# Threshold attention and a squared-ReLU FFN: two hand-written step orders of the attention stage replaced by two others

## The chip, the cores and the metric

The kernel runs on one core of one Trainium2 chip. A core has five engines with a queue each: TensorE (PE: matmuls and transposes; its weight loads are shown as PEld), VectorE (DVE), ScalarE (ACT), GpSimd (POOL) and SyncE (SP, which issues nearly all transfers here). Each engine works through its own instructions in the order in which the program gives them and waits, where it must, on semaphores that the other engines or transfers raise. The metric is the device time of one execution in microseconds (us); the times before were taken in 3 runs.

## The reference

```python
# q, k, v: (8, 8, 576, 64) float32; tau = 0.02
scores = scale * np.matmul(q, k.transpose(0, 1, 3, 2))
thresh = np.max(scores, axis=-1, keepdims=True) - tau
scores = np.where(scores >= thresh, scores, -1000000000.0)
scores = scores - np.max(scores, axis=-1, keepdims=True)
attn = np.exp(scores)
attn = attn / (np.sum(attn, axis=-1, keepdims=True) + 1e-09)
x = np.matmul(attn, v)             # rearranged to (4608, 512)
h = np.maximum(x @ w_in, 0.0)      # w_in (512, 2048)
out = h * h @ w_out                # w_out (2048, 512)
```

`w_in` and `w_out` arrive as 64-bit floats and are turned into 32-bit floats on the chip, with integer operations on the two halves of each number.

## The kernel before

The attention stage comes first (to about 500 us), then two layers of the FFN, whose matrix products use a scheme of sums and differences of blocks that saves multiplications. The change touches the attention stage alone.

**Units and periods.** 8 batches by 4 pairs of heads give 32 pairs; a pair has 576 queries in four tiles of 128 and one of 64, and the last tiles of two pairs share one unit: 144 units of 128 queries. A *period* p handles two units, A and B, of two heads each (j = 0 and 1), so there are 72 full periods with a few partial ones around them. The work is a software pipeline: a period makes the scores and softmax weights of its own units, transposes most of the weights of the period before (fills V and W), the rest of the weights of the one before that (fill U), and multiplies those with the values (PV).

**Steps.** A period is a list of short names, and the function `period` runs the step of each name in the order of the list. Each step appends its instructions to the queues of its engines, so the list sets the order on every engine at once; what stands in different queues is held together by the waits alone (the whole is under a manual schedule). The names:

| step | engine | what it does | line before |
|---|---|---|---|
| SA, SB | PE | scores of unit A and the last 64 keys of both; scores of B, into PSUM `sc` | L434 |
| T | PE | transposes of queries or keys to come, into two banks of `sc` | L398 |
| eT | ACT | copies these out; SP then loads later queries or keys | L403, L411 |
| U, V, W | PE | transposes of softmax weights (W also spreads the reciprocal sums, L515) | L380 |
| eU, eV, eW | ACT | copies these out | L523 |
| PV | PE | weights by values, into banks 0 and 5 of `sc` | L532 |
| topA0 ... topB1 | DVE | reads 576 scores from PSUM, writes them to SBUF, keeps the extreme of each row | L452 |
| leastA, leastB | POOL | adds tau to that extreme (128x2) | L459 |
| powA0 ... powB1 | ACT | exponential | L462 |
| maskA0 ... maskB1 | DVE | compares scores with the threshold, multiplies with the exponentials, sums rows; both inputs in SBUF | L467 |
| over | POOL | adds 1e-9 to the row sums of the period before (needs its last mask) | L474 |
| inv | DVE | reciprocal of these (128x4) | L477 |
| x | DVE in plain periods, ACT in converting ones | takes the product from PSUM (two instructions) | L659, L657 |
| xm | POOL in converting periods | multiplies x with the reciprocals (L669); in all periods, SP's stores of x and loads of values | L669, L578 |
| fetch | SP | loads a chunk of 64-bit weights | L191 |
| c1 | ACT | first step of the conversion of a chunk | L205 |
| c2, c3 | POOL | second and third, on the two halves | L212, L219 |
| c4, c5 | DVE | fourth and fifth, one period later | L227, L235 |
| c6 | POOL | adds the halves (needs c5) | L245 |
| s1, s2 | POOL | one sum of weight blocks each, 128x512 (a few of x at the end) | L122, L125 |

Chunks begin in periods 2 to 33, and a chunk's second half of steps falls in the next period, so periods 2 to 34 are *converting* and use the list `CONVERTING`; the others use `PLAIN`. In plain periods the steps c1 to c6 and fetch do nothing. s1 and s2 do something only from period 36 on: s2 to period 59, s1 until its sums are done (44 of weights and 12 of x, so until period 67). Periods 0 and 1 have lists of their own.

**What sets the order around it.** Besides the waits on data, `touch` adds waits between engines that use the same PSUM bank, so that, for instance, a top in bank 1 waits for the transposes T that the list has put ahead of it in that bank. The masks wait for their exponential and for least; V waits for all masks of the period before; W waits for inv and for the tops of B; the next SA waits for x, the next SB for eW.

Of the kernel before, what the change touches and what calls it, by code (L numbers as in the profile page):

```python
# [48 lines left out]
def kernel(  # L49
# [438 lines left out]
    for g in range(2, 2 * len(pairs)):  # L488
        two, x = divmod(g - 4, 4)
# [99 lines left out]
    def begun(n):  # L589
        return starts.get(n)  # L590

    PLAIN = """
        SA c3 T topA0 over U eU s1 SB topA1 powA1 leastA topB0 powB0 c1 s2 PV c4 V fetch
        inv powA0 c5 topB1 powB1 eT maskA1 x xm W eV maskA0 leastB c2 c6 eW maskB0
        maskB1
    """.split()
    CONVERTING = """
        fetch SA U eU T SB topA0 s1 c1 topA1 topB0 c3 V PV leastA over powA0 topB1
        powA1 powB0 c4 eT inv x maskA1 maskA0 W leastB maskB0 c5 eV c2 powB1 c6 eW maskB1 xm
    """.split()  # L600

    BEGIN_WITH = {
# [740 lines left out]
```

## Time and profile before

| what | value |
|---|---|
| three runs | 1298.58, 1299.42 (median), 1301.99 us |
| profiled execution | span 1298.2 us from the first to the last instruction; of its own time only this span is shown |
| busy share of the span | PE 98%, PEld 86%, DVE 78%, POOL 71%, ACT 65% |
| granted TensorE clock | mean 0.997; 1.00 from 25 us on |
| converting periods 3 to 34 begin (topA0) | 30.03 to 250.54 us |
| plain periods 36 to 59 begin | 263.72 to 415.21 us; period 60 at 421.66 |
| last mask ends | 500.15 us |

A row of the page gives the line, engine, operation, tiles and shapes, the count, then busy time in us and the mean duration of one in ns, then the idle time of the engine just before them. A timeline gives start, duration, engine, line, operation. On DVE a recorded duration overlaps the start of the next instruction, so the pace of a chain is read from start to start. The rows of DVE_READ_ACCUMULATOR belong to the top or mask before them.

### The profile page before, as it was taken

How to read it: one execution, taken by the hardware profiler on the slowest of the kernel's cores; microseconds unless marked ns; L12 is line 12 of the kernel's file. 1: busy time of each engine (PE TensorE's matmuls, PEld its weight loads, DVE VectorE, ACT ScalarE, POOL GpSimd, SP SyncE). 2: the span in 40 equal slices, each digit the busy share in tenths (PEclk: the TensorE clock that was granted, in tenths of full speed). 3: DMA queues.
4: the chain of work that ended last, by engine and by line, in shares of the span. 5: the costliest groups of instructions: out<-in, count | busy, mean ns of one | idle time of the engine just before them, and what ended most of it. 6: DMA issues, size and time to landing. Idle time of an engine off the chain costs nothing.

```text
span 1298.2 us, 45819 instructions
## 1 busy us (share of the span) xinstructions
PE 1276.4 (98%) x18287; PEld 1117.7 (86%) x18287; DVE 1007.0 (78%) x2423; ACT 845.5 (65%) x1498; POOL 926.8 (71%) x1031
## 2 busy tenths in 40 slices
PE   8999999999999999999999999999999999999998
PEld 5777777677777778988888888999999999999998
DVE  6999999999999996886887878867646654665463
ACT  6999999888998984666765856675523432343240
POOL 2787878755555321888897989858787767777775
PEclk8999999999999999999999999999999999999999
DMA  5665566544333312667768768589554224522411
GB/s 143 163 160 154 153 192 180 149 103 110 85 79 80 92 34 64 191 183 218 212 186 226 218 175 235 162 304 391 195 159 164 83 86 159 163 80 88 160 34 34
DMA packets 291413, 196.20 MB, mean 151 GB/s; under 512 B 100096, under 2 KB 252160, under 8 KB 291200
## 3 DMA queue, kind: packets, MB, share of 16 engines
q1 hardware_dynamic: 289888, 192.87, 51.5%
q8 instruction: 144, 2.36, 0.8%
q14 instruction: 69, 0.57, 0.2%
q10 hardware_dynamic: 1312, 0.41, 0.1%
HBM read 120.85 MB, written 72.35 MB: 149 GB/s over the span
## 4 chain that ended last, share of the span: by engine, by line
PE 86%; ACT 5%; DVE 4%; DMA 3%; issue 2%; POOL 0%; SPq 0%; ACTq 0%; DVEq 0%; POOLq 0%
PE po L1077 28%; PE ph L935 16%; PE sc L532 11%; PE sc L434 10%; PE ph L942 10%; PE pt L380 6%; DVE arena L452 2%; PE sc L515 2%; PE sc L398 2%; ACT arena L462 1%; ACT arena L523 1%; DMA g<-arena 1%; PE sc L380 1%; DVE arena L125 1%; DMA wall<-w 1%
## 5 line engine op out<-in xcount | busy, mean ns | idle before, releaser
L125 POOL TENSOR_TENSOR arena<-arena 128x512 f32<-128x512 f32 (+1 forms) x314 | 378.1, 1222 | 147.0 <-DVE arena L125 119.3
L1077 PE MATMUL po<-wall,arena 128*128 128x128 f32 x3528 | 395.0, 275 | 1.9 <-ACT arena L752 1.4
L1077 PEld LDWEIGHTS po<-wall,arena 128*128 128x128 f32 x3528 | 394.4, 192 | 2.5 <-ACT arena L752 1.8
L125 DVE TENSOR_TENSOR arena<-ph,arena 128x512 f32<-128x512 f32 x378 | 255.1, 689 | 79.9 <-PE ph L935 31.5
L122 POOL TENSOR_TENSOR arena<-arena 128x128 f32<-128x128 f32 (+1 forms) x322 | 265.4, 825 | 23.0 <-DMA arena<-w 6.6
L935 PE MATMUL ph<-arena,wall 128*128 128x256 f32 x1176 | 256.6, 380 | 1.8 <-DVE arena L125 1.4
L935 PEld LDWEIGHTS ph<-arena,wall 128*128 128x128 f32 x1176 | 222.2, 190 | 35.9 <-DVE arena L125 5.4
L125 DVE TENSOR_TENSOR arena<-po,arena 128x128 f32<-128x128 f32 x378 | 108.2, 290 | 167.7 <-PE po L1077 163.4
L467 DVE SCALAR_TENSOR_TENSOR arena<-arena 128x576 f32<-128x576 f32 x288 | 235.7, 855 | 0.9 <-ACT arena L462 0.9
L791 ACT COPY c<-arena 128x512 f32<-128x512 f32 (+1 forms) x295 | 169.0, 578 | 71.8 <-DVE arena L122 35.8
L452 DVE TENSOR_SCALAR_CACHE_REDUCE arena<-sc 128x576 f32<-128x576 f32 x288 | 205.1, 748 | 10.9 <-ACT arena L523 4.3
L462 ACT ACTIVATE arena<-arena 128x576 f32<-128x576 f32 x288 | 208.7, 773 | 7.4 <-DVE arena L452 4.2
L532 PEld LDWEIGHTS sc<-arena 64*64 64x64 f32 x5760 | 159.2, 133 | 36.5 <-DVE arena L452 19.8
L532 PE MATMUL sc<-arena 64*64 64x128 f32 (+1 forms) x5760 | 180.5, 262 | 2.9 <-DVE arena L452 1.3
L434 PE MATMUL sc<-arena 64*64 64x64 f32 (+1 forms) x2304 | 176.2, 415 | 3.8 <-ACT arena L403 2.4
L523 ACT COPY arena<-pt 128x1024 f32<-128x1024 f32 x144 | 146.4, 1016 | 27.9 <-PE pt L380 26.5
L122 DVE TENSOR_TENSOR arena<-arena,c 128x512 f32<-128x512 f32 x235 | 154.4, 666 | 11.0 <-ACT c L791 7.6
L752 ACT COPY arena<-po 128x128 f32<-128x128 f32 x63 | 16.6, 264 | 186.4 <-PE po L1077 183.7
L942 PE MATMUL ph<-arena,wall 128*128 128x128 f32 x1176 | 132.0, 275 | 0.7 <-DVE arena L659 0.7
L942 PEld LDWEIGHTS ph<-arena,wall 128*128 128x128 f32 x1176 | 131.6, 192 | 1.1 <-issue 0.8
L380 PEld LDWEIGHTS pt<-ident,arena 64*128 64x128 f32 x2304 | 83.5, 139 | 40.0 <-ACT arena L523 30.1
L434 PEld LDWEIGHTS sc<-arena 64*64 64x64 f32 x2304 | 74.0, 134 | 42.2 <-issue 14.1
(54 smaller groups left out, 1079.7 us busy)
## 6 DMA issues: line engine op xcount, KB each, us to landing
arena<-g SPq DMA_DIRECT2D x144, 256.0 KB, 4.4
g<-arena SPq DMA_DIRECT2D x192, 128.0 KB, 2.9
w<-arena SPq DMA_DIRECT2D x60, 256.0 KB, 2.8
wall<-w SPq DMA_DIRECT2D x49, 256.0 KB, 5.2
g<-arena SPq DMA_DIRECT2D x48, 256.0 KB, 3.8
arena<-w SPq DMA_DIRECT2D x44, 256.0 KB, 3.3
arena<-in_v_dram SPq DMA_DIRECT2D x32, 288.0 KB, 3.8
out_dram<-arena SPq DMA_DIRECT2D x70, 128.0 KB, 2.2
```

Source lines behind the costliest of these rows:

```text
L122: e.tensor_tensor(out=out, in0=x, in1=y, op=ALU.subtract)
L125: e.tensor_tensor(out=out, in0=x, in1=y, op=ALU.add)
L380: made = nc.tensor.transpose(pt[:, r, ts(slot, HALF)], of[rows, :], ident[rows, rows])
L434: made = nc.tensor.matmul(sc[at, ds(to, count)], lhs, kT[rows, ds(at_k, count)], start=True, stop=True)
L452: made = nc.vector.tensor_scalar(out=s[:, j, :], in0=sc[:, ds(at, S)], scalar1=1.0, scalar2=None, op0=ALU.mult, op1=ALU.min, accum_out=nmx ...
L462: nc.scalar.activation(out=w[:, :, j, :], in_=of(j), func=AF.Exp, bias=nmx[:, j : j + 1], scale=-1.0)
L467: nc.vector.scalar_tensor_tensor(out=w[:, :, j, :], in0=of(j), scalar=thr[:, j : j + 1], in1=w[:, :, j, :], op0=ALU.is_le, op1=ALU.mult, a ...
L532: made = nc.tensor.matmul(sc[ds(u * D, D), ds(5 * j * BANK + row, count)], loaded_v[i][rows, (c - (u != j)) % CH, :], wT[m][rows, ds(weigh ...
L791: nc.scalar.copy(c, y)
L935: nc.tensor.matmul(to[:, 2 * j : 2 * j + 2, :], W_IN[m, k][:, ts(2 * h + j, P)], part_x(steps, k, m), start=(not more and j == 0), stop=Tr ...
L942: nc.tensor.matmul(to[:, j, :], W_IN[m, k][:, ts(j, P)], x, start=(not more and j == 0), stop=True, skip_group_check=True,)
L1077: nc.tensor.matmul(to, g[:, j, :], w[:, j, :], start=(not more and j == 0), stop=(j == 3), skip_group_check=True)
```

## The change

The lists `PLAIN` and `CONVERTING` get another order. Both hold the same steps as before, none is added or left out, and no step does anything else than it did. (All lines of the kernel behind the lists move up by three.)

```diff
     PLAIN = """
-        SA c3 T topA0 over U eU s1 SB topA1 powA1 leastA topB0 powB0 c1 s2 PV c4 V fetch
-        inv powA0 c5 topB1 powB1 eT maskA1 x xm W eV maskA0 leastB c2 c6 eW maskB0
-        maskB1
+        s1 T SA topA0 U topA1 leastA SB eU powA1 PV topB0 over powA0 V topB1 eT maskA1 powB0 inv powB1 maskA0 W eV x s2 leastB maskB0 xm maskB1 eW fetch c4 c5 c6
     """.split()
     CONVERTING = """
-        fetch SA U eU T SB topA0 s1 c1 topA1 topB0 c3 V PV leastA over powA0 topB1
-        powA1 powB0 c4 eT inv x maskA1 maskA0 W leastB maskB0 c5 eV c2 powB1 c6 eW maskB1 xm
+        fetch SA U eU T SB c1 s1 topA0 V powA0 topA1 leastA powA1 PV c4 topB0 powB0 topB1 eT maskA0 c3 x over inv leastB maskA1 c2 c5 W maskB0 eV c6 powB1 xm maskB1 eW
     """.split()
```

The new PLAIN list names c4 to c6 but not c1 to c3, which do nothing there. Read engine by engine (c steps left out in plain periods, where they are empty):

| engine | plain before | plain after |
|---|---|---|
| PE | SA T U SB PV V W | T SA U SB PV V W |
| DVE | topA0 topA1 topB0 inv topB1 maskA1 x maskA0 maskB0 maskB1 | topA0 topA1 topB0 topB1 maskA1 inv maskA0 x maskB0 maskB1 |
| ACT | eU powA1 powB0 powA0 powB1 eT eV eW | eU powA1 powA0 eT powB0 powB1 eV eW |
| POOL | over s1 leastA s2 leastB | s1 leastA over s2 leastB |

| engine | converting before | converting after |
|---|---|---|
| PE | SA U T SB V PV W | the same |
| DVE | topA0 topA1 topB0 topB1 c4 inv maskA1 maskA0 maskB0 c5 maskB1 | topA0 topA1 c4 topB0 topB1 maskA0 inv maskA1 c5 maskB0 maskB1 |
| ACT | eU c1 powA0 powA1 powB0 eT x eV powB1 eW | the same |
| POOL | c3 leastA over leastB c2 c6 xm | leastA c3 over leastB c2 c6 xm |

## The prediction

> **What bounds the kernel now.** I read first the busy time of the engines in two stretches of the attention stage, then the groups of instructions by form in the same stretches, then the timelines of VectorE (DVE) and GpSimd (POOL) in single periods. The granted clock is 1.00 in both stretches.
>
> ```profile
> core 0: us, PE busy (x) PEld busy (x) DVE busy (x) ACT busy (x) POOL busy (x), PEclk, DMA share, GB/s
> 30.00:235.00 205.00, 201.27 (x4952) 150.72 (x4946) 204.39 (x549) 197.71 (x357) 163.53 (x201) 1.00 0.64 168
> 257.00:408.00 151.00, 149.02 (x3926) 111.76 (x3930) 146.03 (x438) 136.22 (x213) 87.01 (x115) 1.00 0.41 95
> ```
>
> In the converting stretch DVE is never idle: its chain sets the period, 7.07 us from one topA0 to the next in most of them (107.76 to 114.85, say). In the plain stretch TensorE is the busier (149.02 of 151), and DVE idles 5 us. From topA0 of period 36 (263.72) to that of period 60 (421.66) are 24 periods of 6.58.
>
> So what counts is what makes a DVE step longer. The masks are not equally long in the two stretches:
>
> ```profile
> L467 DVE SCALAR_TENSOR_TENSOR arena<-arena 128x576 f32<-128x576 f32 x116 | 101.0, 905 | 0.6 <-ACT arena L462 0.6
> ...
> L467 DVE SCALAR_TENSOR_TENSOR arena<-arena 128x576 f32<-128x576 f32 x149 | 116.0, 815 | 0.0
> ```
>
> The timeline of one converting period tells why (DVE first, then POOL):
>
> ```profile
> 103.83 0.78 DVE L467 SCALAR_TENSOR_TENSOR arena<-arena 128x576 f32<-128x576 f32 x1
> ...
> 104.54 1.20 DVE L467 SCALAR_TENSOR_TENSOR arena<-arena 128x576 f32<-128x576 f32 x1
> ...
> 105.68 0.81 DVE L467 SCALAR_TENSOR_TENSOR arena<-arena 128x576 f32<-128x576 f32 x1
> ...
> 106.42 0.69 DVE L235 SCALAR_TENSOR_TENSOR arena<-arena 128x512 int32<-128x512 int32 x1
> 107.02 0.81 DVE L467 SCALAR_TENSOR_TENSOR arena<-arena 128x576 f32<-128x576 f32 x1
> ...
> 104.06 2.02 POOL L212 TENSOR_SCALAR arena<-arena 128x512 int32<-128x512 uint32 x1
> 107.25 1.48 POOL L245 TENSOR_TENSOR wall<-arena 128x512 int32<-128x512 int32 x1 [1.18 <-DVE arena L235]
> ```
>
> c2 (L212) starts 0.23 after maskA1, and it is the next mask, begun while c2 is under way, that takes 1.20 for 0.81: it is held 0.40. c6 (L245) starts 0.23 after maskB1, and maskB1 keeps its 0.81. So who is first at the port goes first, and the other waits. Two more rows give sizes. In period 2 a mask starts 0.215 behind xm (L669) and takes 1.13, held 0.32; in a plain period maskA1 starts 0.95 after a sum of weights (L122) and is held 0.14, so that L122 holds a mask off until about 1.09 after its own start:
>
> ```profile
> 28.97 1.13 DVE L467 SCALAR_TENSOR_TENSOR arena<-arena 128x576 f32<-128x576 f32 x1 [0.61 <-ACT arena L462]
> ...
> 28.75 0.73 POOL L669 TENSOR_TENSOR arena<-arena 128x256 f32<-128x256 f32 x1
> ...
> 306.15 0.95 DVE L467 SCALAR_TENSOR_TENSOR arena<-arena 128x576 f32<-128x576 f32 x1
> ...
> 305.20 1.28 POOL L122 TENSOR_TENSOR wall<-wall 128x512 f32<-128x512 f32 x1
> 306.46 0.80 POOL L459 TENSOR_SCALAR arena<-arena,tau_p 128x2 f32<-128x2 f32 x1
> ```
>
> The last row is leastB: begun 0.18 behind a mask's usual start it takes 0.80 where it takes 0.29 beside a top, so POOL waits for masks likewise. The tops read PSUM, and POOL work beside them costs neither anything. Durations overlap the next instruction; below I go from start to start: top 0.68, mask 0.74, c5 0.60, c4 0.34, inv 0.09, x 0.47 with the read of the accumulator before it.
>
> The Trainium skill ("SBUF — State Buffer", section "SBUF: two separate sides") has this as an exclusive lock on a port pair that DVE and GpSimd share, held for the whole instruction. The trace agrees on who waits but not on how long: c2 lasted 1.54 beyond the start of the held mask and held it 0.40, and L122 let go 0.2 before its recorded end.
>
> **The change, converting periods (2 to 34).** PE and ACT keep their order; no instruction is added. SP's queue keeps its order (fetch, the loads of eT, the store of c6, the stores and loads of xm).
>
> 1. c4 moves ahead of topB0 (0.34): it is on DVE's chain before and after, so 0. topB1, leastB and eT come 0.34 later, which ACT covers: powB1 then ends about 6.0 into the period, and maskB1 starts at 6.3 or later.
> 2. c3 moves behind leastA on POOL. It reads what c1 wrote; over follows it and is done 1.45 after topA1, while inv, which waits for it, comes 2.4 after. 0.
> 3. maskA0 is first, then inv, maskA1, c5, maskB0, maskB1. With M the start of maskA0: leastB waits for maskA0 and ends at M+0.97 (the 0.80 row), c2 starts at about M+1.05, maskA1 at M+0.83. c2 waits for maskA1, as now, and holds what is next, c5 instead of a mask: 0.40 again, M+1.54 to M+2.54. No net cost. I take c5 as no different from a mask; the gain if it is not held is 0.40 a period.
> 4. c5 now stands before maskB0, so c6 no longer waits for c5 but for c2's end on POOL. c2 ends 1.54 after the start of the step that it held, M+3.08, and POOL's next starts 0.08 later (28.67 to 28.75 in period 2): M+3.16. maskB0 runs M+2.54 to M+3.28, and maskB1 would start at M+3.28. c6 is there 0.12 earlier, and maskB1 is held. Price: xm's 0.32 is the lowest row (half as wide). L122's 1.09 less the head start of 0.12 gives 0.97 as highest. The c6 of now, begun during a mask, ends 0.97 after that mask's successor starts, less the 0.2: 0.77. I take 0.80, nearest that row. Periods 3 to 34: 32 x 0.80 = **25.6 us** (10 to 31).
>
> V, which needs maskB1, and PV come later by the same, with DVE leading; xm then waits for maskB1 and runs beside the next topA0: 0.
>
> **Plain periods (35 to 72).** On PE, T goes before SA: both precede topA0 now as well, since topA0 waits for T's bank: 0. On ACT, powA0 and eT go ahead of powB0 and powB1, which then end about 4.2 and 4.9 into the period; maskB0 and maskB1 come at 4.8 and 5.5 at the earliest: 0. inv behind maskA1 delays the last part of W to about 4.0 into the period, when PE is still at V: 0. x behind maskA0 ends 4.8 in, and SA, with T before it, starts at 5.3: 0. Loads and stores keep their order on SP; xm's come 1 us later, with a ring of two x tiles and three v tiles to cover it.
>
> On POOL the order becomes s1, leastA, over, s2, leastB. Now over, which waits for maskB1, stands first and keeps s1 and s2 beside the tops. After, nothing that s1 waits for comes from DVE, so it follows the previous leastB straight away, into the masks; s2 is behind leastA and over.
>
> 1. s2 against maskA1: leastA starts 0.18 after topA1, takes 0.26 to the next start, over 0.31: s2 starts 0.75 after topA1; maskA1 comes two tops after, at 1.36, that is 0.61 into s2, and is held until 1.09: 0.48, or 0.40 without the gap of 0.08 before s2. I take 0.45 (0.14, the row above, to 0.67, L122's whole duration).
> 2. s1 against maskB0: leastB ends 0.97 after maskA1's real start; maskA0, at 0.83, is ahead of s1 by 0.11 to 0.2 and runs unhindered. s1 gets its turn when maskA0 ends, and maskB0 comes 0.47 later (x between reads PSUM). By the blocked c6, POOL lets go 0.76 after that end: held 0.29; by L122's 1.09, 0.62. I take 0.40; should s1 pass maskA0 instead, it would hold that up to 1.09.
>
> DVE's own work is 2.71 + 0.09 + 2.96 + 0.47 and 0.05 for the last accumulator read = 6.28; with 0.85 it is 7.13, over TensorE's 6.58, which takes up the first 0.30. Periods 36 to 59 have both sums: 24 x 0.55 = 13.2. Periods 60 to 67 have s1 alone (6.68): about 1. Together **14 us** (5 to 24).
>
> The rest of the kernel is the same instructions in the same order, later. The page's span is 1298.2, the median 1299.42; its surroundings, 1.2, stay. 1299.4 + 25.6 + 14 = **1339 us**.
>
> By the skill's rule, a lock until POOL's instruction ends, c6 would cost 0.97, s2 0.67 and s1 about 0.5: 31 + 21, 1351. That is an estimate from the rows with the rule's ending; it lies inside the first case below, and since c2's 0.40 speaks against it I give it 0.05 of that case's 0.52.
>
> **Rivals.**
> - c6 comes too late: M+3.16 against M+3.28 is a margin of 0.12, and leastB's small step could shift either side. If maskB1 is first, as now, the converting periods stay at 7.1 and only the plain stage pays: 1313.
> - Faster: c5 is not held by c2. The two rows with c5 beside c2's tail show no delay (0.68), but they begin 1.7 after c2's start. Then c5 hides c2, each of 31 periods loses 0.40 (12.4 us), and maskB1 starts at M+2.88, ahead of c6. It decides when the sums cost under 8 us: with the lower bound in plain, 1299.4 - 12.4 + 5 = 1292. Against it: c5 reads two SBUF operands as a mask does. The skill's "GPSIMD Engine Reference" (section "8. Key points") names two SBUF inputs as what contends; no row here shows it for c5.
> - The move does nothing: POOL's work only waits and never holds DVE. Both stages stay, TensorE's chain still sets 6.58: 1299 to 1301. Against it speak the 0.40 of all but a few converting periods.
>
> **How the numbers follow.** Both collisions 0.52 (1339, its own range 1314 to 1355); c6 misses 0.24 (1304 to 1323); c5 immune 0.14 (of it faster 0.10, same 0.02, slower 0.02); nothing 0.10 (faster 0.03, same 0.05, slower 0.02). Below 1301 lies most of the last two, about 0.2: the range is 1301 to 1355. 0.3% (3.9 us) is about what can be told from no change: faster 0.13, same 0.07, slower 0.80.
>
> **What would show it.** Converting: c5 near 1.07 instead of 0.68, maskB1 near 1.6, no mask at 1.20 besides, a period of 7.9. Plain: maskA1 near 1.25, maskB0 near 1.2, L122 starting beside masks with 1.9 recorded, DVE without idle time. Wrong: maskB1 at 0.81 with c6 behind it, or c5 at 0.68.

## The result, and the profile after

The changed kernel takes 1347.96 us (median of 4 runs, 1345.61 to 1349.94); the kernel before took 1299.63 beside it (4 runs). The ratio is 1.0362, with a 95% interval of 1.0341 to 1.0382: slower by 48 us. The forecast was 1339, with 1301 to 1355 as its range. The profiled execution has a span of 1345.8 against 1298.2, 47.6 longer, and all of it lies in the attention stage: the last mask ends at 547.73 instead of 500.15, 47.6 later, and what follows takes the same time as before.

By the starts of topA0 the 47.6 split like this (us; after the first column each number is a difference of two such starts):

| stretch | before | after | more | forecast |
|---|---|---|---|---|
| converting, start of period 3 to start of 35 | 227.19 | 253.94 | 26.8 | 25.6 |
| plain with s1 and s2, 36 to 60 | 157.94 | 176.07 | 18.1 | 13.2 |
| plain with s1 alone, 60 to 68 | 52.77 | 54.78 | 2.0 | about 1 |

The rest, 0.7, is in period 35 and the last periods. The busy time of the engines in the two stretches, for the kernel after (start and end of the stretch, its length, then busy time with the number of instructions for PE, PEld, DVE, ACT and POOL, the granted clock, the share of the DMA engines and GB/s):

```profile
30.00:235.00 205.00, 190.11 (x4478) 137.35 (x4472) 205.00 (x493) 179.10 (x320) 164.81 (x180) 1.00 0.57 149
290.00:466.00 176.00, 169.04 (x4132) 127.67 (x4124) 175.86 (x457) 140.66 (x222) 104.46 (x120) 1.00 0.35 80
```

The clock is 1.00 in both, so nothing is lost there. DVE is now busy without a gap in the plain stretch too, 175.86 of 176, and TensorE, which set the pace there, has 7 us of idle time. In the converting stretch DVE was the bound and stays it. DVE has no more to do than it had; its instructions last longer. The groups by form, the first two rows from the converting stretch of the kernel after (30 to 235 us), the last from its plain stretch (291 to 466 us):

```profile
L467 DVE SCALAR_TENSOR_TENSOR arena<-arena 128x576 f32<-128x576 f32 x104 | 101.2, 989 | 0.6 <-ACT arena L462 0.6
...
L235 DVE SCALAR_TENSOR_TENSOR arena<-arena 128x512 int32<-128x512 int32 x26 | 30.9, 1189 | 0.0
...
L467 DVE SCALAR_TENSOR_TENSOR arena<-arena 128x576 f32<-128x576 f32 x95 | 103.2, 1102 | 0.0
```

The masks have gone from a mean of 905 to 989 ns and from 815 to 1102, and c5 (L235) is at 1189, where a single c5 took 0.69 before. In the chain that ended last the same shift is seen: DVE's share of it goes from 4% to 11%, PE's from 86% to 79%.

```profile
PE 79%; DVE 11%; issue 5%; ACT 3%; DMA 2%; POOL 0%; DVEq 0%; SPq 0%; ACTq 0%; POOLq 0%
```

Which instructions are long is read in the timeline of the kernel after, DVE first and then POOL (start, duration, engine, line, operation). One converting period:

```profile
112.67 0.81 DVE L467 SCALAR_TENSOR_TENSOR arena<-arena 128x576 f32<-128x576 f32 x1
...
113.50 0.78 DVE L467 SCALAR_TENSOR_TENSOR arena<-arena 128x576 f32<-128x576 f32 x1
...
114.21 1.20 DVE L235 SCALAR_TENSOR_TENSOR arena<-arena 128x512 int32<-128x512 int32 x1
115.34 0.81 DVE L467 SCALAR_TENSOR_TENSOR arena<-arena 128x576 f32<-128x576 f32 x1
...
116.07 1.58 DVE L467 SCALAR_TENSOR_TENSOR arena<-arena 128x576 f32<-128x576 f32 x1
...
113.71 2.10 POOL L212 TENSOR_SCALAR arena<-arena 128x512 int32<-128x512 uint32 x1
115.89 1.14 POOL L245 TENSOR_TENSOR wall<-arena 128x512 int32<-128x512 int32 x1
117.00 1.24 POOL L666 TENSOR_TENSOR arena<-arena 128x256 f32<-128x256 f32 x1
```

c6 (L245) is on POOL at 115.89 and maskB1 on DVE at 116.07: c6 is first by 0.18, and maskB1 takes 1.58 where it took 0.81. c2 (L212) now holds c5, which goes from 0.69 to 1.20, and no mask besides maskB1 is long. The plain periods are as regular. Period 42:

```profile
337.43 1.39 DVE L467 SCALAR_TENSOR_TENSOR arena<-arena 128x576 f32<-128x576 f32 x1
...
338.85 0.78 DVE L467 SCALAR_TENSOR_TENSOR arena<-arena 128x576 f32<-128x576 f32 x1
...
339.96 1.42 DVE L467 SCALAR_TENSOR_TENSOR arena<-arena 128x576 f32<-128x576 f32 x1
...
336.25 0.29 POOL L459 TENSOR_SCALAR arena<-arena,tau_p 128x2 f32<-128x2 f32 x1 [2.82 <-DVE arena L452]
336.63 0.23 POOL L474 TENSOR_SCALAR arena<-arena 128x4 f32<-128x4 f32 x1
336.94 1.27 POOL L122 TENSOR_TENSOR wall<-wall 128x512 f32<-128x512 f32 x1
338.19 0.79 POOL L459 TENSOR_SCALAR arena<-arena,tau_p 128x2 f32<-128x2 f32 x1
338.95 1.81 POOL L122 TENSOR_TENSOR wall<-wall 128x512 f32<-128x512 f32 x1
```

s2 (the first L122) begins 0.49 before maskA1, which takes 1.39. s1 (the second) is queued at 338.95, 0.10 behind maskA0; it is recorded with 1.81 because it waits until maskA0 is done, and then maskB0 at 339.96 has to wait for it and takes 1.42. maskA0 and maskB1 are unhindered.

### The profile page after: what moved, and what is told of

It reads as the page before. It is cut to its first block, busy times and chain, and to the rows that moved or that the text cites. A ratio compares the mean times of both kernels' runs of the same rounds, so it can differ in the third digit from the quotient of the medians.

```text
span 1345.8 us, 45999 instructions
## 1 busy us (share of the span) xinstructions
PE 1303.0 (97%) x18287; PEld 1131.6 (84%) x18287; DVE 1060.4 (79%) x2423; ACT 844.5 (63%) x1498; POOL 965.7 (72%) x1031
## 4 chain that ended last, share of the span: by engine, by line
PE 79%; DVE 11%; issue 5%; ACT 3%; DMA 2%; POOL 0%; DVEq 0%; SPq 0%; ACTq 0%; POOLq 0%
PE po L1074 28%; PE ph L932 16%; PE sc L434 10%; PE ph L939 9%; DVE arena L452 7%; PE sc L532 6%; PE pt L380 5%; PE sc L515 2%; PE sc L398 2%; DVE arena L467 1%; DMA g<-arena 1%; ACT arena L462 1%; ACT c L788 1%; ACT arena L523 1%; DVE arena L125 1%
## 5 line engine op out<-in xcount | busy, mean ns | idle before, releaser
L122 POOL TENSOR_TENSOR arena<-arena 128x128 f32<-128x128 f32 (+1 forms) x322 | 270.0, 840 | 26.8 <-DMA arena<-w 10.4
L467 DVE SCALAR_TENSOR_TENSOR arena<-arena 128x576 f32<-128x576 f32 x288 | 283.6, 1002 | 0.9 <-ACT arena L462 0.9
L462 ACT ACTIVATE arena<-arena 128x576 f32<-128x576 f32 x288 | 211.9, 776 | 44.3 <-DVE arena L452 44.3
L459 POOL TENSOR_SCALAR arena<-arena,tau_p 128x2 f32<-128x2 f32 x144 | 80.9, 562 | 183.3 <-DVE arena L452 179.4
L532 PEld LDWEIGHTS sc<-arena 64*64 64x64 f32 x5760 | 156.9, 133 | 59.6 <-DVE arena L452 56.3
L532 PE MATMUL sc<-arena 64*64 64x128 f32 (+1 forms) x5760 | 185.1, 262 | 16.8 <-DVE arena L452 15.9
L434 PE MATMUL sc<-arena 64*64 64x64 f32 (+1 forms) x2304 | 181.7, 417 | 2.8 <-DVE arena L656 1.2
L122 DVE TENSOR_TENSOR arena<-arena,c 128x512 f32<-128x512 f32 x235 | 154.1, 665 | 10.8 <-ACT c L788 8.2
```

The costliest lines, as they stand in the source:

```text
L122: e.tensor_tensor(out=out, in0=x, in1=y, op=ALU.subtract)
L434: made = nc.tensor.matmul(sc[at, ds(to, count)], lhs, kT[rows, ds(at_k, count)], start=True, stop=True)
L462: nc.scalar.activation(out=w[:, :, j, :], in_=of(j), func=AF.Exp, bias=nmx[:, j : j + 1], scale=-1.0)
L467: nc.vector.scalar_tensor_tensor(out=w[:, :, j, :], in0=of(j), scalar=thr[:, j : j + 1], in1=w[:, :, j, :], op0=ALU.is_le, op1=ALU.mult, a ...
L532: made = nc.tensor.matmul(sc[ds(u * D, D), ds(5 * j * BANK + row, count)], loaded_v[i][rows, (c - (u != j)) % CH, :], wT[m][rows, ds(weigh ...
```

## Experiments

**The theory.** DVE and POOL hold each other up where a POOL instruction meets a DVE instruction whose two inputs both lie in SBUF (a mask, c5); whoever is there first goes first. Three places in the lists put POOL first: c5 ahead of maskB0 (which lets c6 in ahead of maskB1), over behind leastA in plain periods (which lets s2 and s1 in among the masks), and, by a price set at nothing, c4. **The rivals.** The time comes from the rest of the reorder (the other order on ACT and PE, maskA0 first, x behind the masks); or from DVE's own order, whatever POOL does; or c6 was late anyway and something else lengthens maskB1. So the runs put back one place at a time, do one place alone on the kernel before, change the length of the instruction that holds, and make the rest of the change without the three places.

The stretches of all of them, from the same starts of topA0 (us):

| kernel | periods 3 to 35 | 36 to 60 | 60 to 68 | ratio to before, 95% |
|---|---|---|---|---|
| before | 227.19 | 157.94 | 52.77 | |
| after | 253.94 | 176.07 | 54.78 | 1.0362 (1.0341 to 1.0382) |
| after, c5 back behind maskB0 | 233.09 | 176.15 | 54.52 | 1.0206 (1.0190 to 1.0221) |
| before, c5 ahead of maskB0 | 250.78 | 157.80 | 53.02 | 1.0173 (1.0157 to 1.0188) |
| after, c6 in two halves | 240.84 | 176.14 | 54.54 | 1.0264 (1.0247 to 1.0281) |
| after, over first in plain periods | 254.55 | 157.92 | 52.96 | 1.0214 (1.0199 to 1.0230) |
| before, POOL's plain order of after | 226.11 | 180.56 | 55.35 | 1.0201 (1.0182 to 1.0220) |
| after, c5 back and over first | 233.75 | 157.90 | 52.94 | 1.0054 (1.0034 to 1.0075) |
| after, c5 and c4 back | 224.80 | 176.07 | 54.79 | 1.0159 (1.0143 to 1.0175) |
| before, without c2 | 223.51 | 158.64 | 52.76 | 0.9993 (0.9983 to 1.0004) |
| before, new converting list with c4, c5 back | 224.76 | 157.73 | 52.73 | 0.9990 (0.9979 to 1.0001) |
| the same, and new plain list with over first | 226.21 | 158.06 | 52.74 | 0.9993 (0.9984 to 1.0002) |

### c5 back behind maskB0

```diff
     CONVERTING = """
-        ... maskA0 c3 x over inv leastB maskA1 c2 c5 W maskB0 eV c6 powB1 xm maskB1 eW
+        ... maskA0 c3 x over inv leastB maskA1 c2 W maskB0 c5 eV c6 powB1 xm maskB1 eW
```

> The changed kernel with one name moved: in the converting list c5 goes back behind maskB0. Theory (GpSimd's c6, no longer waiting for c5, gets its turn just ahead of maskB1 and holds it): c2 then holds maskB0 by 0.40 instead of c5, c6 again waits for c5 and starts inside maskB1, which returns from 1.58 to 0.81 recorded; the converting period falls from 7.95 to 7.08, and the time by 32 x 0.83, to about 1321 us. Rival (the early c4, maskA0 ahead of maskA1, or c3 behind leastA costs the time): these stay, and the time stays near 1348; anything between shows a share of each.

Measured: 1327.10 us, and the converting stretch gives back 20.9 of its 26.8. The timeline of this kernel, DVE and then POOL:

```profile
207.03 0.58 DVE L227 TENSOR_SCALAR arena<-arena 128x512 int32<-128x512 int32 x1
...
210.43 1.28 DVE L467 SCALAR_TENSOR_TENSOR arena<-arena 128x576 f32<-128x576 f32 x1
...
211.65 0.68 DVE L235 SCALAR_TENSOR_TENSOR arena<-arena 128x512 int32<-128x512 int32 x1
212.25 0.81 DVE L467 SCALAR_TENSOR_TENSOR arena<-arena 128x576 f32<-128x576 f32 x1
...
206.61 0.72 POOL L666 TENSOR_TENSOR arena<-arena 128x256 f32<-128x256 f32 x1
207.32 0.46 POOL L459 TENSOR_SCALAR arena<-arena,tau_p 128x2 f32<-128x2 f32 x1
...
212.48 1.48 POOL L245 TENSOR_TENSOR arena<-arena 128x512 int32<-128x512 int32 x1 [0.42 <-DVE arena L235]
```

c6 waits for c5 again and comes 0.23 behind maskB1, which is back at 0.81; c2 holds maskB0 instead of c5. That is the theory. But all periods but the first and the last are 7.23 to 7.34 long, not 7.07, and the expected 1321 is missed by 6. The reason stands in the first row: c4 (L227) in its new place, between topA1 and topB0, runs into xm (L666, to 207.33); it is recorded with 0.58 and takes 0.51 from start to start where it took 0.34. The move that was priced at nothing costs something once xm is on time.

### c5 ahead of maskB0, on the kernel before

```diff
     CONVERTING = """
-        powA1 powB0 c4 eT inv x maskA1 maskA0 W leastB maskB0 c5 eV c2 powB1 c6 eW maskB1 xm
+        powA1 powB0 c4 eT inv x maskA1 maskA0 W leastB c5 maskB0 eV c2 powB1 c6 eW maskB1 xm
```

> The kernel before with one name moved: in its converting list c5 goes ahead of maskB0, all else as before. Theory: c6 now waits for c5 in the middle of maskB0, is next in turn, and holds maskB1 by 0.77; period 7.84 instead of 7.07, 32 x 0.77 = 25 us, 1324 us. Rival (only together with c4's and maskA0's new places does c6 meet maskB1, or the loss is theirs): the time stays at 1300 us.

Measured: 1322.13 us; the converting stretch is 23.6 longer. A period is 7.85; the 1.3 that is missing to 25 is in two long periods of the kernel before, which this one does not have. The timeline of this kernel, DVE and then POOL:

```profile
104.76 0.69 DVE L235 SCALAR_TENSOR_TENSOR arena<-arena 128x512 int32<-128x512 int32 x1
105.36 0.81 DVE L467 SCALAR_TENSOR_TENSOR arena<-arena 128x576 f32<-128x576 f32 x1
...
106.10 1.58 DVE L467 SCALAR_TENSOR_TENSOR arena<-arena 128x576 f32<-128x576 f32 x1
...
105.60 1.47 POOL L245 TENSOR_TENSOR wall<-arena 128x512 int32<-128x512 int32 x1 [0.41 <-DVE arena L235]
```

Here one exchange of two neighbours, in a list that is otherwise the old one, gives maskB1 the same 1.58. c6 is ready during maskB0, takes its turn when that ends, and maskB1 comes behind it. So the converting loss needs neither the new order of maskA0 and maskA1 nor anything else of the new list; the rival that lays it on the rest falls for this stretch.

### c6 in two halves

```diff
-        nc.gpsimd.tensor_tensor(out=a, in0=hi, in1=lo, op=ALU.add)
+        for part in (ds(0, WC // 2), ds(WC // 2, WC // 2)):
+            nc.gpsimd.tensor_tensor(out=a[:, part], in0=hi[:, part], in1=lo[:, part], op=ALU.add)
```

> The changed kernel with c6 as two additions of 256 columns in place of one of 512; the same work in the same places. Theory (a GpSimd instruction that has its turn holds the mask for about its own length, and the mask goes in between two of them): the first half holds maskB1 by some 0.36 (0.53 for a 256-wide addition, as xm showed, less its head start of 0.17) instead of 0.78, the second waits for maskB1's end and runs beside topA0; the converting period falls from 7.95 to about 7.55, the time by 13, to 1335 us. Rival one (maskB1 waits for c6's result or place by a semaphore) and rival two (the second half wins over the waiting mask too): no gain, 1348 to 1352 us.

Measured: 1334.09 us. The timeline of this kernel (all its lines behind L245 are one higher than in the kernel after):

```profile
103.70 1.16 DVE L468 SCALAR_TENSOR_TENSOR arena<-arena 128x576 f32<-128x576 f32 x1
...
103.55 1.78 POOL L246 TENSOR_TENSOR wall<-arena 128x256 int32<-128x256 int32 x2
```

maskB1 starts 0.15 behind the first half and goes from 1.58 to 1.16: it is held 0.35 instead of 0.77, goes in between the halves, and the second half waits for it (the two together are recorded with 1.78). The list is unchanged here, so maskB1's length follows the length of the POOL instruction in front of it, which no order on DVE, ACT or PE would explain.

### over first in plain periods

```diff
     PLAIN = """
-        s1 T SA topA0 U topA1 leastA SB eU powA1 PV topB0 over powA0 V topB1 ...
+        over s1 T SA topA0 U topA1 leastA SB eU powA1 PV topB0 powA0 V topB1 ...
```

> The changed kernel with one name moved: in the plain list over goes to the front, so that s1 stands behind a step that waits for maskB1. T before SA, the new order of the exponentials, inv behind maskA1 and x behind maskA0 stay. Theory (the sums of weights s1 and s2 hold maskB0 and maskA1): s1 runs beside topA0 and topB0 again and maskB0 returns to 0.81; s2 starts 2.0 after topA0 and lets go at 3.08, while maskA1 comes at 2.72, so up to 0.36 of maskA1's hold stays. DVE's chain is then 6.3 to 6.64 a period against TensorE's 6.58, and the time falls by 17 to 20, to 1328 to 1331 us. Rival (the order on TensorE, ScalarE or VectorE costs the plain stage its 0.75 a period): 1347 us, as no queue but GpSimd's is changed.

Measured: 1327.14 us, and the plain stretch from 36 to 60 is 157.92 long where that of before is 157.94: all 18.1 are back by the place of one 128x4 addition of 0.23 us. The expectation left up to 0.36 of maskA1's hold in place; none is left, since s2 starts 1.12 ahead of maskA1 (324.71 against 325.83) and a sum holds until about 1.09. This kernel from 291 us on, its busy times first (to 416) and then its group of masks (to 447):

```profile
291.00:416.00 125.00, 124.72 (x3268) 94.68 (x3261) 118.82 (x362) 109.71 (x177) 71.94 (x96) 1.00 0.40 91
```

```profile
L467 DVE SCALAR_TENSOR_TENSOR arena<-arena 128x576 f32<-128x576 f32 x95 | 75.0, 809 | 0.0
```

TensorE is the bound again (124.72 of 125), DVE idles 6, and the masks have a mean of 809. The new order on PE, ACT and DVE is still in this kernel, so none of it costs anything in plain periods.

### POOL's plain order of after, on the kernel before

```diff
     PLAIN = """
-        SA c3 T topA0 over U eU s1 SB topA1 powA1 leastA topB0 powB0 c1 s2 PV c4 V fetch
+        s1 SA c3 T topA0 U eU SB topA1 powA1 leastA over topB0 powB0 c1 s2 PV c4 V fetch
```

> The kernel before with GpSimd's order of the changed plain list alone (s1 first, over behind leastA); TensorE, VectorE and ScalarE keep their order. Theory, with VectorE's order of before: inv, between topB0 and topB1, waits 0.2 for over; s2 starts 0.86 after topA1 and holds maskA1 0.3; leastB follows, s1 starts while x reads PSUM, is ahead of maskA0 and holds it 0.8. VectorE's chain is 6.28 + 1.3 = 7.6 a period against 6.58: 24 x 1.0 + 8 x 0.7 = 30 us, 1330 us, and it is maskA0, not maskB0, that grows. Rival (GpSimd's order costs only together with the new order of the other engines): 1300 us.

Measured: 1323.63 us; 36 to 60 is 22.6 longer, 60 to 68 is 2.6 longer. The timeline of this kernel, DVE and then POOL:

```profile
302.23 1.19 DVE L467 SCALAR_TENSOR_TENSOR arena<-arena 128x576 f32<-128x576 f32 x1
...
303.75 1.69 DVE L467 SCALAR_TENSOR_TENSOR arena<-arena 128x576 f32<-128x576 f32 x1
305.37 0.81 DVE L467 SCALAR_TENSOR_TENSOR arena<-arena 128x576 f32<-128x576 f32 x1
...
301.53 1.27 POOL L122 TENSOR_TENSOR wall<-wall 128x512 f32<-128x512 f32 x1
302.78 0.79 POOL L459 TENSOR_SCALAR arena<-arena,tau_p 128x2 f32<-128x2 f32 x1
303.54 1.28 POOL L122 TENSOR_TENSOR wall<-wall 128x512 f32<-128x512 f32 x1
```

With DVE's old order the sums meet other masks: s2 holds maskA1 (1.19), and s1, which starts 0.21 ahead of the mask behind x, holds that one, maskA0, for 0.88 (1.62 from start to start). POOL's order alone makes the plain loss, and it is larger here than in the change. The loss is 25.5 us where 30 was expected: the period is 7.52, not 7.6 (22.6 us in place of 24), and the periods with s1 alone lose 2.6 and not 5.6. The rest of the distance to 1330 is the kernel before, which took 1298.12 beside it and not 1300.

### c5 back and over first

```diff
     PLAIN = """
-        s1 T SA topA0 U topA1 leastA SB eU powA1 PV topB0 over powA0 V topB1 ...
+        over s1 T SA topA0 U topA1 leastA SB eU powA1 PV topB0 powA0 V topB1 ...
     CONVERTING = """
-        ... leastB maskA1 c2 c5 W maskB0 eV c6 powB1 xm maskB1 eW
+        ... leastB maskA1 c2 W maskB0 c5 eV c6 powB1 xm maskB1 eW
```

> The changed kernel with both moves: over to the front of the plain list, c5 back behind maskB0 in the converting list. Everything else of the change stays. Theory (the two collisions are separate and are the loss): the gains of the two single moves, 20.9 and 20.8 us, add up, to about 1306 us; the 6 us left over the kernel before are c4's hold by leastA and xm (next run). Rival (one loss hides the other, so that they overlap): well above 1310.

Measured: 1305.47 us. The two losses add up: the stretches are those of the two single runs (233.75 against 233.09, 157.90 against 157.92). What is left over the kernel before, 6.6 in the converting stretch, is laid on c4; the next run and the last one put c4 back.

### c5 and c4 back

```diff
     CONVERTING = """
-        ... powA1 PV c4 topB0 powB0 topB1 eT maskA0 c3 x over inv leastB maskA1 c2 c5 W maskB0 eV c6 ...
+        ... powA1 PV topB0 powB0 topB1 c4 eT maskA0 c3 x over inv leastB maskA1 c2 W maskB0 c5 eV c6 ...
```

> The changed kernel with c5 back behind maskB0, and c4 back behind topB1 too. With c5 alone back, the converting period was 7.32 and not 7.08: c4, now behind topA1, starts while GpSimd is at xm and leastA, and takes 0.50 from start to start for 0.34, and the c2-held maskB0 took 0.07 more. Theory (c4 is held by xm, 0.16 a period): 32 x 0.16 = 5 us less than with c5 alone back, 1322 us. Rival (the rest is maskA0's place ahead of maskA1, or c3's): still 1327.

Measured: 1318.82 us, 8.3 below the run with c5 alone put back, where 5 were expected (by the ratios to the kernel before, which was 2 us faster beside this run, it is 6), and the converting stretch is 8.3 shorter (224.80 against 233.09). A period is 7.00, less than the 7.07 of before. The timeline of this kernel, DVE and then POOL:

```profile
103.33 0.81 DVE L467 SCALAR_TENSOR_TENSOR arena<-arena 128x576 f32<-128x576 f32 x1
...
104.08 0.17 DVE L477 RECIPROCAL arena<-arena 128x4 f32<-128x4 f32 x1
104.17 1.10 DVE L467 SCALAR_TENSOR_TENSOR arena<-arena 128x576 f32<-128x576 f32 x1
...
103.18 0.39 POOL L459 TENSOR_SCALAR arena<-arena,tau_p 128x2 f32<-128x2 f32 x1
103.65 1.96 POOL L212 TENSOR_SCALAR arena<-arena 128x512 int32<-128x512 uint32 x1
```

With c4 in front of the masks, leastB is done soon after maskA0 starts, and c2 is queued during maskA0. It gets its turn when maskA0 ends at 104.08; DVE's next is inv, 0.09 long, and then maskA1 takes 1.03 to the next start, where a mask behind inv takes 0.71: held 0.32, not 0.40 as before, nor 0.48 as maskB0 in the run with c5 alone put back. The short inv uses up a part of the hold.

### c2 left out, on the kernel before

```diff
+    nought = const.tile([P, 512], FP32, name="nought")
+    nc.vector.memset(nought, 0.0)
...
-            nc.gpsimd.tensor_scalar(out=lo, in0=lo.bitcast(U32), scalar1=2.0**-29, scalar2=None, op0=ALU.mult)
+            if isinstance(m, tuple):
+                nc.gpsimd.tensor_scalar(out=lo, in0=lo.bitcast(U32), scalar1=2.0**-29, scalar2=None, op0=ALU.mult)
...
-        nc.gpsimd.tensor_tensor(out=a, in0=hi, in1=lo, op=ALU.add)
+        nc.gpsimd.tensor_tensor(out=a, in0=hi, in1=nought[:, :].bitcast(I32), op=ALU.add)
```

The lower halves of the 64-bit weights are dropped here; c6 adds a tile of zeros. The condition keeps c2 in the conversions of the later stage, which pass a tuple.

> The kernel before with c2 left out in the converting periods, and c6 adding a tile of zeros in place of what c2 made: so the lower halves of the weights are dropped from the conversion. Nothing else is changed. Theory (c2 holds maskA0 by 0.40 in nearly every converting period): maskA0 falls from 1.20 to 0.81, and VectorE's chain from 7.07 to 6.67; ScalarE, busy 6.8 of each 7.07, is then the next bound, so the period is 6.7 to 6.85 and the time 8 to 12 us less, 1288 to 1292. Rival (the mask is slow for another reason, a wait for leastA or an exponential): maskA0 stays at 1.20 and the time at 1300.

Measured: 1297.44 us, a ratio of 0.9993 whose interval takes in 1: a miss, where 8 to 12 us less were expected. The mask is back at 0.81 in most periods, so c2 is what held it, but a period goes only from 7.07 to 6.88. The busy times of this kernel in the converting stretch:

```profile
30.00:235.00 205.00, 201.69 (x5017) 153.55 (x5013) 199.81 (x556) 198.30 (x362) 134.01 (x177) 1.00 0.64 171
```

DVE now idles 5 us, and PE (201.69) and ACT (198.30) are as near to the bound as DVE: 0.2 of the 0.4 were to be had at all. c6 with the tile of zeros also takes 1.81 instead of 1.48, and two periods with a late chunk of weights (8.54 and 9.12 long) took back some 3.5 us (the kernel before has 1.3 of that kind). In the trace the converting stretch is 3.7 shorter; the median of the runs shows 0.7. So this run shows the mechanism, and bounds what removing c2's hold is worth; it does not price it.

### The rest of the change

First the new converting list with c4 and c5 put back, beside the old plain list; then the same with the new plain list, over first. The second is the whole change without its three places.

```diff
     CONVERTING = """
-        fetch SA U eU T SB topA0 s1 c1 topA1 topB0 c3 V PV leastA over powA0 topB1
-        powA1 powB0 c4 eT inv x maskA1 maskA0 W leastB maskB0 c5 eV c2 powB1 c6 eW maskB1 xm
+        fetch SA U eU T SB c1 s1 topA0 V powA0 topA1 leastA powA1 PV topB0 powB0 topB1 c4 eT maskA0 c3 x over inv leastB maskA1 c2 W maskB0 c5 eV c6 powB1 xm maskB1 eW
```

> The kernel before with the changed converting list alone, c4 and c5 put back as in the last run but one (c4 behind topB1, c5 behind maskB0); the plain list is that of before. In that run the converting period was 7.00 against 7.07 of before, as c2 now has its turn when maskA0 ends, inv (0.09) comes next and maskA1 is held 0.30 instead of maskA0's 0.40. Theory: 30 x 0.07 = 2 us less than before, ratio 0.998 (0.996 to 1.000). Rival (the 7.00 came with the plain list or is the chip's): ratio 1.000 or above.

```diff
     PLAIN = """
-        SA c3 T topA0 over U eU s1 SB topA1 powA1 leastA topB0 powB0 c1 s2 PV c4 V fetch
-        inv powA0 c5 topB1 powB1 eT maskA1 x xm W eV maskA0 leastB c2 c6 eW maskB0
-        maskB1
+        over s1 T SA topA0 U topA1 leastA SB eU powA1 PV topB0 powA0 V topB1 eT maskA1 powB0 inv powB1 maskA0 W eV x s2 leastB maskB0 xm maskB1 eW fetch c4 c5 c6
```

> The same converting list with the changed plain list and over at its front: all of the change but the three places of c4, c5 and over. Theory: no GpSimd instruction holds a mask in the plain stage, TensorE sets 6.58 a period there as it does in the kernel before, so it ends with the run beside it, ratio 0.996 to 1.001 to the kernel before. Rival (the new order on TensorE, VectorE or ScalarE costs or gains something of its own in the plain stage): it differs from the run beside it by more than 3 us.

Measured: 1296.35 (0.9990, 0.9979 to 1.0001) and 1296.81 us (0.9993, 0.9984 to 1.0002). Both converting lists have periods of 7.00, which would be 2 us less than before; in the second kernel two periods with late chunks (8.14 and 8.38) cost 2.5, in the first one such period (8.09) 1.1, and in the kernel before two cost 1.3. Neither can be told from the kernel before. So the whole of the 48 us lies in the three places of c5, over and c4, and what is left of the change, maskA0 first included, is worth nothing that these runs can measure. No version here beats the kernel before beyond doubt.

## Why the prediction was right, and where its sizes were off

**Converting, step 4 (c6 holds maskB1): right, in place and size.** The margin on which it hung, c6 0.12 ahead of maskB1, was 0.18 (115.89 against 116.07); with maskA0 at 112.67, c6 came at M+3.22 and maskB1 at M+3.40. That the margin held has some luck in it: c6 was 0.06 later than forecast, and maskB1 0.12 later, because c5 was held longer than forecast; with c5 held 0.40, and c6 where it was, the margin would have been about 0.06. maskB1 is held 0.77 where 0.80 was taken, 24.6 us in 32 periods where 25.6 stood. The row that I chose, c6's own 1.48 begun during a mask, was the right one; L122's 1.09 would have given 0.97. The run on the kernel before and the one with halves show the cause. The rival "c6 comes too late" falls.

**Converting, step 3 (c2 holds c5 as it held a mask): right in kind, a little small.** c5 goes from 0.60 to between 1.06 and 1.16 from start to start, held 0.46 to 0.56 and not 0.40. The rival "c5 immune" falls with it. The 0.1 more per period, 3 us, and the 24.6 make 27.8; the stretch shows 26.8, since two long periods of before (7.37 and 8.10, each with a late chunk: ACT waits 0.28 and 1.64 for its transfer in front of c1) have no counterpart after: 1.3 less.

**Converting, step 1 (c4: 0): right in the sum, wrong by itself.** I had followed only what comes later through c4's move, and not what runs on POOL beside its new place. In the change xm is itself delayed by c6 and maskB1 (117.00 to 118.24) and is over when c4 comes, so c4 is as short as before and costs nothing:

```profile
118.94 0.41 DVE L227 TENSOR_SCALAR arena<-arena 128x512 int32<-128x512 int32 x1
```

With c5 put back, xm ends 0.30 into c4, which loses 0.17 from start to start. Putting c4 back gains 0.31 a period there (7.31 to 7.00), 0.17 of it c4's and most of the rest c2's, which holds 0.32 in place of 0.48; over the stretch it is 8.3 us, since one period with a late chunk (8.12) takes 1.1 back. One collision was hiding another.

**Plain, steps 1 and 2: both collisions where they were expected, both too small; a third of the 20 us was missed.** The term "s2 starts 0.75 after topA1" failed: it was 0.86 (336.08 for topA1, then leastA 0.17 later, over 0.38 after that, s2 0.31 after over). I had taken leastA at its 0.26 to the next start, as it stands ahead of a sum; ahead of over it is 0.38. So maskA1 was 0.49 into s2 and not 0.61. That s2 lets go 1.09 after its start was right: 336.94 + 1.08 = 338.02, and 338.02 + 0.74 is the end at 338.76. Held 0.59, not 0.45. For s1 the wrong row was chosen: between the blocked c6's 0.76 and L122's 1.09 I took the middle, and it was 1.01 (maskA0 ends at 339.56, maskB0 ends at 341.31, 0.74 before that is 340.57). The two instructions are not alike: L122 is recorded with 1.27 when it runs free, c6 with 1.04, in one period of the run with c5 and c4 put back where DVE is idle when c6 starts:

```profile
232.84 1.04 POOL L245 TENSOR_TENSOR arena<-arena 128x512 int32<-128x512 int32 x1 [0.43 <-DVE arena L235]
```

So maskB0 was held 0.61, not 0.40. In the other direction, DVE's own work was 6.13 and not 6.28: x takes 0.40, the mask behind inv 0.71, and the 0.05 that was added for the last accumulator read did not come on top. So 7.33 stood in place of 7.13, and 24 x 0.2 is the 4.9 us by which the term of 13.2 fell short. TensorE did go off the bound, as forecast: its 6.58 lies inside the 7.33.

**The steps at nothing.** T before SA, the order of the exponentials, inv and x behind the masks, c3 behind leastA: the last run holds all of them and equals the kernel before. The rival "nothing" falls through the three places, but for the rest of the change it was right.

**The Trainium skill's rule** ("SBUF — State Buffer", section "SBUF: two separate sides"), one shared port pair that the first comer keeps for its whole instruction, came to 1351 and so nearer to the total than my 1339. Its two sums do not do so for their own reasons: c6 would have cost 0.97 (0.77 measured), s2 0.67 (0.59), s1 about 0.5 (0.61). For the adds the measured end of the hold is 0.19 before the recorded end (L122 1.08 of 1.27, c6 0.95 of 1.14, a part of which it spends behind maskB0), so the rule holds for them but for that last piece. For c2 it does not: 0.5 of c5's delay against the 1.60 that c2 still lasts after c5's start.

**What stays open.** That order of arrival decides is shown, and for the adds also that their length sets the price; for c2, which lasts longer than any add, it does not. That the place where they meet is a port to SBUF is only argued: the tops and x, which read PSUM, are never held beside POOL (a top is recorded with at most 0.77, whatever POOL does), while masks, c5 and c4 are; no run moved an operand to other memory. Why c4 is held with one input in SBUF and x with one is not stays open too; c4 passes its 512 columns in 0.34 us where c5 takes 0.60, and whether that is the reason was not tested. Why c2 lets go so much sooner than the adds was not followed.

## What to carry to other kernels

Where VectorE and GpSimd both work from SBUF, read who is queued at the moment when each such VectorE instruction ends: whichever is waiting goes next and the other pays. Here an add of GpSimd kept VectorE out for all but its last 0.2 us, c2 for only 0.4 to 0.6 of its 2 us, so the price has to be read from a row of the same instruction; and a forecast needs the arrival times to 0.1 us, not the busy times. Put GpSimd's long instructions where VectorE reads PSUM, and look for the small instructions that keep them there: here an addition of 0.23 us (over) and one exchange of two VectorE steps (c5) were the gates, worth about 20 us each. Price a moved step by what runs on the other engine beside its new place, also when what it delays is covered.

## What was not expected of the hardware

- A hold can be divided and partly hidden. Two adds of 256 columns in place of one of 512 let the mask in between (held 0.35 instead of 0.77), and where a reciprocal of 0.09 stood between two masks, the second was held 0.32 instead of 0.40.
- An instruction of VectorE with one SBUF input can be held as well: c4, an integer shift and mask by two constants, took 0.51 instead of 0.34 beside xm. x, which has one input in SBUF and one in PSUM, was not held beside s1 (0.40 for its two instructions).
- The time from one GpSimd start to the next depended on what followed: from leastA (128x2) it was 0.26 to a 128x512 sum and 0.38 to the 128x4 addition. Why was not followed.
- With collisions in every period the stage runs more evenly than without: periods 37 to 58 are 7.32 to 7.34 after, 6.51 to 6.75 with over first, and 6.35 to 7.15 before.
